# Fused attention and MLP forward and backward: the copy of turned e in block 0, q's column in parts, K's turn and k's maximum at other places, six buffers of h1

## Chip, cores and metric

One core of a Trainium2 chip runs the whole program in one launch. The metric is the device time of one execution in microseconds. Before the change the median of three runs is 2354.04 us (2353.44 to 2355.04).

## What is computed

The kernel computes an attention branch and an MLP branch on one normalized input, gates one with the other, and returns the output and the gradients of seven inputs for a given `grad_out`. Sequence 2048, width 512, 32 heads of 16, MLP width 1792, bfloat16 in and out.

```python
xn = layernorm(x)
q, k, v = split_heads(xn @ wqkv)                     # 32 heads of 16
s = (softmax(q @ k.T * 0.25) @ v) @ wo               # attention branch
g = silu(gelu(layernorm(xn) @ w1 + b1) @ w2 + b2)    # MLP branch
out = x + s * g
_, vjp = jax.vjp(f, x, wqkv, wo, w1, b1, w2, b2); grads = vjp(grad_out)
```

## The kernel before

The program has three parts: a preparation (`phase_pre`, about 0 to 175 us), the attention forward and backward together (`attention_core`, about 175 to 1970 us), and the rest of the backward pass (`phase3`).

**Preparation, first half.** Rows are normalized and projected to q, k and v in 16 tiles of 128 rows (groups `g` of four tiles). For each tile of k the squares are made on GpSimd (`norms`, L174, tile `sq`) and summed on VectorE (L175, `kn`).

**Preparation, second half**, written in the order of its engines' queues (`manual_schedule` for PE, ACT, DVE and POOL; SP's order is left to the scheduler):

- `h_tile(g, fc)`: one tile of h = y w1 in the turned layout, four matmuls (L264) for each of 4 groups and 14 chunks `fc`. The bias is added on DVE (L267) or ACT (L269) into one half of a pair tile `h1p`, of which there are four buffers. After each second chunk ACT makes the gelu of the pair (L271), and SP stores h1 and gelu(h1) (L272 `H1T_s`, L273 `HGT_s`). A buffer of `h1p` comes free when its store has landed.
- `q_norm(t)`: the squared norm of a row of q per head, squares on POOL (L174, `sq` from `NQ`), sum on DVE (L175, `qn`). Sixteen of them are strewn between the h tiles of groups 1, 2 and 3.
- k's maximum: `reduce_max` over k's norms on DVE (L457) and a `partition_all_reduce` on POOL (L458), in group 1 behind `h_tile(1, 0)`. The reduction needs another code library on POOL than the squares do: one `MODIFY_POOL_CONFIG` stands ahead of it and one ahead of the next `sq`.
- `m_group(g)`: the second MLP matmul for four row tiles (L282, 14 matmuls each), its addition of the bias on DVE (L286), sigmoid on ACT (L289, L290), and five DVE operations (L294 to L309) that give the gate's products, stored from POOL's queue (L310).
- `do_proj`, `do_done`: the gradient of the attention output (L345, L346), copied into the padded operand `QPad` (L353) and stored (L356).
- `row_shift()`: from q's norms and k's maximum a bound of each row of scores, the square root on ACT (L437), the first column of `NQ` on DVE (L438), the copy into `QPad` on POOL (L440), two DMA transposes of `QPad` into `QDT` (L426, `turn_q`, for blocks 0 and 1), the store of `NQ` (L443, 2176 KB), and the copy `NATQq` (L444). A one-element Exp (L471) behind the square root brings the exponential's table in.

Two DMAs of SP's queue matter besides: K's turn (L450, `KPad` into `KVT`, written behind `h_tile(0, 8)`), and the load of `b2` (L247), for whose conversion on POOL (L248) the queue of POOL waits.

**Attention.** 16 pairs of heads times 4 blocks of queries make 64 blocks of 16 steps. A step `g` has `s` (scores, L887), ACT's Exp to `et` (L915, called S), `d` (L909, two matmuls, one for each head, each with one PSUM buffer), the products `m1` and `m0` of `d` and `et` on DVE (L926, tile `gts`), and the sums `a1` (L946, L949) and `a2` (L959). A quarter of the exponentials for the other layout is had by turning `et` on TensorE (`E`, L871, tile `ET` in the one PSUM buffer `z`) and copying it on DVE (`eE`, L876) instead of a second Exp.

The order on PE, ACT and DVE is a written list (`PE_ORDER`, `DVE_ORDER`), but block 0 has its own from `first_block`: there is no block before it, so the last quarter of `m_group` work is done in its gaps (`left_over`: tiles 12 to 15 of the MLP product, then the rest of the `do` projections, L411, and one turn, L402). On PE step `g` of block 0 is s(g+2), [E(g-1) at g = 4, 8 and 12], d(g+1), a1(g), V, a2(g-1), W(g). V and W are the places of the left-over work: W(0) to W(7) are the halves of the products of tiles 12 to 15 (seven matmuls each, in the buffer `z`), W(8), W(9), W(11), W(12) are `do` projections. On DVE a left-over tile has its bias addition (L286), `rest1` (L294, L295, L304) and `rest2` (L308, L309). The lists are merged by a loop that gives out an instruction as soon as what it needs has been given out:

```python
            if g % 4 == 0 and g and g // 4 - 1 in turned:
                p.append(("E", g - 1))
                v.append(("eE", g - 1))
            p += [("d1", g + 1), ("d0", g + 1), ("a1", g), ("V", g)]
```

From block 1 on the written lists hold, and nothing of the change reaches them.

Of the kernel before, what the change touches and what calls it, by code (L numbers as in the profile page):

```python
# [41 lines left out]
def phase_pre(ctx, tc, k, A_x, A_wqkv, A_wo, B_w1, B_b1, B_w2, B_b2, grad_out, opnds, psz, tailp):  # L42
# [210 lines left out]
    def h_tile(g, fc):  # L253
        if fc == 0 and g < 3:
            hgT[g] = p2.tile([128, FC, 512], bf16, name="hgT")[:]
        elif fc == 0:
            hgT[g] = k.dQall[:].rearrange("p t d -> p (t d)")[:, 0:FC * 512].rearrange("p (c s) -> p c s", c=FC)
        if fc % 2 == 0:
            if g or fc:
                h1ps.append(p2.tile([128, 2, 512], bf16, name="h1p", bufs=4))  # L260
        h1p = h1ps[-1]
        ps = psA.tile([128, 512], f32, name="ps_h1", tag="mm")
        for ic in range(IC):
            nc.tensor.matmul(ps[:], lhsT=w1_sb[:, ic, fc * 128:(fc + 1) * 128], rhs=yT[g][:, :, ic, :],  # L264
                             start=(ic == 0), stop=(ic == IC - 1))
        if fc % 2 == 0 or fc in (5, 11):
            nc.vector.tensor_scalar(out=h1p[:, fc % 2], in0=ps[:], scalar1=b1c[:, fc:fc + 1], scalar2=None, op0=ALU.add)  # L267
# [161 lines left out]
    def q_norm(t):  # L429
        norms(p2, qn2[:, t, :], NQ[:, :, t, :, 1:17])  # L430

    def row_shift():

        nc.vector.tensor_scalar(out=kmax2[:], in0=kmax2[:], scalar1=UINFL, scalar2=None, op0=ALU.mult)
        nc.vector.tensor_tensor(out=qn2[:], in0=qn2[:], in1=kmax2[:].rearrange("p (o h) -> p o h", o=1).to_broadcast([128, NT, H]),
                                op=ALU.mult)
        nc.scalar.activation(out=qn2[:], in_=qn2[:], func=ACT.Sqrt)  # L437
        nc.vector.tensor_scalar(out=NQ[:, :, :, :, 0], in0=qn2[:].rearrange("p t (a j) -> p a t j", j=2), scalar1=-1.0, scalar2=None,  # L438
                                op0=ALU.mult)
        nc.gpsimd.tensor_copy(out=QPad[:, :, 0:2, 0:17], in_=NQ[:, 0])  # L440
        turn_q(0)
        turn_q(1)
        nc.sync.dma_start(out=k.NATQq_s, in_=NQ[:].rearrange("p a t j c -> p a (t j c)"))  # L443
        nc.gpsimd.tensor_copy(out=OP0["NATQq"][:], in_=NQ[:, 0])  # L444

    with tc.manual_schedule(engines={ET_.PE, ET_.Activation, ET_.DVE, ET_.Pool}):
        for fc in range(FC):
            h_tile(0, fc)
            if fc == 8:
                nc.sync.dma_start_transpose(out=OP0["KVT"][:].rearrange("r (m k) -> r m k", m=16), in_=KPad[:].rearrange("q k s c -> q (k s c)"))  # L450
        qn = list(range(NT))
        for fc in range(FC):
            h_tile(1, fc)
            if fc in (2, 4, 7, 9, 12):
                q_norm(qn.pop(0))
            if fc == 0:
                nc.vector.reduce_max(out=kmaxrun[:], in_=kn2[:].rearrange("p t h -> p h t"), axis=AX.X)  # L457
                nc.gpsimd.partition_all_reduce(kmax2[:], kmaxrun[:], channels=128, reduce_op=bass_isa.ReduceOp.max)  # L458
# [339 lines left out]
def attention_core(ctx, tc, opnds, ps_z, tail, NAT_s, NATQ_s, Oall, dQall, dKVT_out, ident_f32, ident_bf, npairs=16, nqc=4, turned=(0, 1, 2)):  # L798
# [265 lines left out]
    def first_block():  # L1064
# [16 lines left out]
    def joined(first, rest):  # L1081
# [197 lines left out]
```

## Time and profile before

| | |
|---|---|
| median of three runs | 2354.04 us (2353.44 to 2355.04) |
| profiled execution | 2355.04 us, its span 2353.3 us |
| busy: PE, DVE, ACT, POOL | 95%, 86%, 87%, 13% of the span |
| mean granted clock of TensorE | 0.985 |
| preparation, up to the first score | 0 to 175 us |
| block 0, up to the first steps of block 1 | 175 to 232 us |

Times are microseconds from the span's start. A line of the timeline gives start, busy time, engine, line, operation, output and inputs, shape and count; in brackets stands the idle time of the engine ahead of it and what ended that. Lines of the same kind close together are merged into one. PEld is the weight load of TensorE; SPq is the issue of a DMA on SP's queue. A line of the windows view gives for one stretch the busy time of PE, PEld, DVE, ACT and POOL with counts, the granted clock of TensorE as a share of full speed, the share of busy DMA, and GB/s.

### The profile page before, as it was taken

What the parts mean: (1) busy time and instruction counts of PE and PEld (TensorE: products, weight loads), DVE (VectorE), ACT (ScalarE), POOL (GpSimd) and SP (SyncE); (2) the same over time, 40 slices, a digit from 0 to 9 for tenths busy, and PEclk for the clock granted to TensorE, in tenths of its full rate; (3) what the DMA queues carried; (4) which work ended last, traced back from release to release, by engine and by line L of the source; (5) the groups of instructions that cost most, each with busy time, mean ns of one, the idle gap of its engine ahead of it and who ended that gap; (6) DMA issues with size and microseconds to landing.
All of it is one profiled execution on the core that took longest, in us unless ns stands there. A gap on an engine that the chain in (4) does not pass through costs nothing.

```text
span 2353.3 us, 50893 instructions
## 1 busy us (share of the span) xinstructions
PE 2235.4 (95%) x20082; PEld 796.2 (34%) x20128; DVE 2024.0 (86%) x3600; ACT 2043.5 (87%) x2329; POOL 314.8 (13%) x757
## 2 busy tenths in 40 slices
PE   7898999999999999999999999999999998889698
PEld 3342333333333333333333333333333333334343
DVE  6576999999999999999999999999999996775164
ACT  6564999999999999999999999999999998883143
POOL 4230111111111111111111111111111112100000
PEclk9998999999999999999999999999999999999799
DMA  9686999999999989999999999999999998796961
GB/s 288 221 276 149 176 170 173 177 165 185 158 189 163 180 163 180 163 180 175 169 177 167 184 163 183 164 179 166 177 167 173 160 155 229 192 205 129 172 161 63
DMA packets 1315362, 415.56 MB, mean 177 GB/s; under 512 B 1272241, under 2 KB 1291698, under 8 KB 1313970
## 3 DMA queue, kind: packets, MB, share of 16 engines
q1 hardware_dynamic: 1311362, 401.56, 90.0%
q0 software_dynamic: 2176, 7.34, 0.9%
q8 instruction: 157, 2.57, 0.4%
q10 hardware_dynamic: 1584, 3.41, 0.4%
q14 instruction: 83, 0.68, 0.1%
HBM read 46.52 MB, written 49.03 MB: 41 GB/s over the span
## 4 chain that ended last, share of the span: by engine, by line
PE 76%; DVE 12%; issue 3%; DMA 3%; ACT 3%; SPq 2%; POOL 0%; ACTq 0%; DVEq 0%; POOLq 0%
PE d L909 12%; PE X L946 11%; PE s L887 11%; PE Z L1027 9%; PE X L959 7%; DVE gts L926 5%; PE Z L1019 5%; PE ET L871 5%; PE t L899 4%; PE XT L971 2%; PE X L949 1%; PE ps_dy L709 1%; PE ps_dwkv L759 1%; PE ps_dw L654 1%; PE ps_m L282 1%
## 5 line engine op out<-in xcount | busy, mean ns | idle before, releaser
L926 DVE TENSOR_TENSOR gts<-d,et 128x512 bf16<-128x512 f32 x2048 | 1322.0, 684 | 77.1 <-issue 25.9
L915 ACT ACTIVATE et<-s 128x1024 bf16<-128x1024 f32 x1024 | 1044.8, 1046 | 11.4 <-PE d L909 11.1
L920 ACT ACTIVATE e<-t 128x1024 bf16<-128x1024 f32 x832 | 867.8, 1044 | 23.1 <-PE t L899 6.2
L909 PE MATMUL d<-QDT,KVT 32*128 32x512 bf16 x2048 | 757.9, 384 | 22.4 <-DVE gts L926 21.3
L887 PE MATMUL s<-QDT,KVT 32*128 32x512 bf16 x2048 | 398.1, 384 | 5.8 <-DMA QDT<-QPad 3.1
L1027 PE MATMUL Z<-gk,W 128*32 128x512 bf16 x2048 | 397.0, 384 | 0.0
L946 PE MATMUL X<-et,Lc 128*32 128x512 bf16 x2048 | 369.8, 388 | 0.0
L949 PE MATMUL X<-et,NAT 128*32 128x512 bf16 x2048 | 368.7, 388 | 0.0
L959 PE MATMUL X<-gts,NAT 128*17 128x512 bf16 x2048 | 330.9, 382 | 0.0
L1019 PE MATMUL Z<-e,W 128*32 128x512 bf16 x1664 | 321.6, 383 | 2.8 <-DVE ob L1046 1.2
L899 PE MATMUL t<-KVT,QDT 32*128 32x512 bf16 x1664 | 323.2, 383 | 1.0 <-ACT e L920 1.0
L909 PEld LDWEIGHTS <-KVT 32*128 32x128 bf16 x2048 | 173.4, 91 | 236.7 <-issue 236.3
L887 PEld LDWEIGHTS <-KVT 32*128 32x128 bf16 x2048 | 105.9, 91 | 251.0 <-issue 227.7
L993 POOL TENSOR_TENSOR W<-NATQd,rL 128x128 bf16<-128x128 bf16 x64 | 25.7, 401 | 1124.7 <-DVE rL L992 1124.7
L1027 PEld LDWEIGHTS <-W 128*32 128x32 bf16 x2048 | 100.2, 94 | 172.5 <-issue 142.2
L1019 PEld LDWEIGHTS <-W 128*32 128x32 bf16 x2048 | 105.4, 94 | 106.6 <-issue 97.3
L899 PEld LDWEIGHTS <-QDT 32*128 32x128 bf16 x1664 | 92.1, 91 | 145.7 <-issue 140.9
L946 PEld LDWEIGHTS <-Lc 128*32 128x32 bf16 x2048 | 83.5, 93 | 165.0 <-issue 164.9
L876 DVE COPY eE<-ET 128x1024 bf16<-128x1024 bf16 x192 | 130.2, 678 | 6.6 <-PE ET L871 6.6
L871 PE MATMUL ET<-ident_bf,et 128*128 128x128 bf16 x1536 | 119.1, 220 | 0.9 <-DVE e L286 0.9
L871 PEld LDWEIGHTS <-et 128*128 128x128 bf16 x1536 | 86.5, 98 | 44.4 <-issue 44.4
L959 PEld LDWEIGHTS <-NAT 128*17 128x17 bf16 x2048 | 79.6, 89 | 59.1 <-issue 42.8
(197 smaller groups left out, 2334.6 us busy)
## 6 DMA issues: line engine op xcount, KB each, us to landing
gk<-gts SPq DMA_TRANSPOSE x512, 4.5
H1T_s<-h1p SPq DMA_DIRECT2D x28, 256.0 KB, 3.7
h<-H1T_s SPq DMA_DIRECT2D x28, 256.0 KB, 3.5
HGT_s<-hgT SPq DMA_DIRECT2D x21, 256.0 KB, 4.3
NAT_s<-NS SPq DMA_DIRECT2D x4, 1056.0 KB, 5.5
dKVT_s<-ob SPq DMA_DIRECT2D x16, 256.0 KB, 3.6
gb<-GB_s SPq DMA_DIRECT2D x4, 1024.0 KB, 6.2
Rkv<-dKVT_s SPq DMA_DIRECT2D x2, 2048.0 KB, 14.7
```

What stands on the lines that cost most here:

```text
L871: nc.tensor.transpose(ET[:, hj, m * 128:(m + 1) * 128], st_et[g - 3 + m][:, hj, 384:512], ident_bf[:])
L887: nc.tensor.matmul(s[:, hj, :], lhsT=op["KVT"][r, kb * 128:(kb + 1) * 128], rhs=op["QDT"][r, qc * 512:(qc + 1) * 512], start=True, stop=Tr ...
L899: nc.tensor.matmul(t[:, hj, :], lhsT=op["QDT"][r, q0:q0 + 128], rhs=op["KVT"][r, kc * 512:(kc + 1) * 512], start=True, stop=True, tile_pos ...
L909: nc.tensor.matmul(d[:], lhsT=op["KVT"][r, kb * 128:(kb + 1) * 128], rhs=op["QDT"][r, qc * 512:(qc + 1) * 512], start=True, stop=True, til ...
L915: nc.scalar.activation(out=et[:], in_=st_s.pop(g)[:], func=ACT.Exp)
L920: nc.scalar.activation(out=e[:], in_=st_t.pop(g)[:], func=ACT.Exp)
L926: nc.vector.tensor_tensor(out=gts[:, g % 2, hj], in0=st_d.pop((g, hj))[:], in1=st_et[g][:, hj], op=ALU.mult)
L946: nc.tensor.matmul(X[64 + 32 * hj:96 + 32 * hj, :], lhsT=Lc[:, :], rhs=et[:, hj, :], start=(kb == 0), stop=False, skip_group_check=True, t ...
L949: nc.tensor.matmul(X[32 * hj:32 * hj + 32, :], lhsT=NATt[:, kb, hj, 1:33], rhs=et[:, hj, :], start=(kb == 0), stop=(kb == 15), tile_positi ...
L959: nc.tensor.matmul(X[64 + 32 * hj:64 + 32 * hj + 17, :], lhsT=NATt[:, kb, hj, 0:17], rhs=gts[:, kb % 2, hj, :], start=False, stop=(kb == 1 ...
L1019: nc.tensor.matmul(Z[32 * hj:32 * hj + 32, :], lhsT=blk[j]["W1"][:, qb, hj, :], rhs=e[:, hj, :], start=(qb == 0), stop=False, tile_positio ...
L1027: nc.tensor.matmul(cur["Z"][32 * hj:32 * hj + 32, :], lhsT=blk[j]["W2"][:, qb, hj, :], rhs=grhs, start=False, stop=(qb == 3), tile_positio ...
```

## The change

- `h1p` has six buffers instead of four.
- k's maximum (`reduce_max` and `partition_all_reduce`) stands behind `h_tile(0, 5)` instead of `h_tile(1, 0)`.
- K's turn is written behind `h_tile(1, 13)` instead of `h_tile(0, 8)`.
- The `q_norm`s are spread 6, 6 and 4 over groups 1, 2 and 3 instead of 5, 5 and 6.
- `row_shift` is split: the two multiplications on DVE behind `h_tile(3, 9)`, the square root behind `h_tile(3, 13)` and so ahead of the last `do_proj` copy, the column of `NQ` and the copy into `QPad` in two parts (tiles 0 to 3, tiles 4 to 15) behind the small Exp, each with its turn. The store of `NQ` is written behind `m_group(2)`.
- In block 0 `eE(g-1)` stands in DVE's list behind the products `m(g)`, not ahead of them.

The order of PE's instructions is the same in both. SP's scheduler puts K's turn at the same place as before, right ahead of the load of `b2`. The store of `NQ` and the reload behind it (L830 before, L837 after) now stand behind the two turns of `QPad`, and ahead of the turn of `dso` (L299). On POOL the reduction's first library now comes right behind the conversion of `b2`, and the two copies into `KPad` for the second pair (L834 and L835 before) come between the squares. In block 0 the loop now gives out m(4), m(8) and m(12) one step earlier: m(4) stands ahead of `rest2` of tile 12 and of the bias addition of tile 13, m(8) ahead of `rest2` of tile 14 and of the bias addition of tile 15.

```diff
-    h1ps = [p2.tile([128, 2, 512], bf16, name="h1p", bufs=4)]
+    h1ps = [p2.tile([128, 2, 512], bf16, name="h1p", bufs=6)]
...
-    def row_shift():
+    def row_shift1():
...
+    def row_shift2():
         nc.scalar.activation(out=qn2[:], in_=qn2[:], func=ACT.Sqrt)
...
-        nc.gpsimd.tensor_copy(out=QPad[:, :, 0:2, 0:17], in_=NQ[:, 0])
-        turn_q(0)
-        turn_q(1)
-        nc.sync.dma_start(out=k.NATQq_s, in_=NQ[:].rearrange("p a t j c -> p a (t j c)"))
+    def row_shift3():
+        for ts in (slice(0, 4), slice(4, 16)):
+            nc.vector.tensor_scalar(out=NQ[:, :, ts, :, 0], in0=qn2[:, ts].rearrange("p t (a j) -> p a t j", j=2), scalar1=-1.0, scalar2=None,
+                                    op0=ALU.mult)
+            nc.gpsimd.tensor_copy(out=QPad[:, ts, 0:2, 0:17], in_=NQ[:, 0, ts])
+            turn_q(ts.start // 4)
...
             h_tile(0, fc)
-            if fc == 8:
-                nc.sync.dma_start_transpose(out=OP0["KVT"][:]...)
+            if fc == 5:
+                nc.vector.reduce_max(out=kmaxrun[:], in_=kn2[:].rearrange("p t h -> p h t"), axis=AX.X)
+                nc.gpsimd.partition_all_reduce(kmax2[:], kmaxrun[:], channels=128, reduce_op=bass_isa.ReduceOp.max)
...
             h_tile(1, fc)
-            if fc in (2, 4, 7, 9, 12):
+            if fc in (2, 4, 6, 8, 10, 12):
                 q_norm(qn.pop(0))
-            if fc == 0:
-                nc.vector.reduce_max(...)
-                nc.gpsimd.partition_all_reduce(...)
+        nc.sync.dma_start_transpose(out=OP0["KVT"][:]...)
...
+                if g == 3 and fc == 9:
+                    row_shift1()
+                if g == 3 and fc == FC - 1:
+                    row_shift2()
                 if fc >= 10:
                     do_proj(4 * (g - 2) + fc - 10)
-                elif fc in (1, 3, 5, 6, 8) or fc == 9 and g == 3:
+                elif fc in (1, 3, 5, 6) or fc in (8, 9) and g == 2:
                     q_norm(qn.pop(0))
...
-        row_shift()
         e_one = ...
+        row_shift3()
         m_group(2)
+        nc.sync.dma_start(out=k.NATQq_s, in_=NQ[:].rearrange("p a t j c -> p a (t j c)"))
...
                 p.append(("E", g - 1))
-                v.append(("eE", g - 1))
...
             v += [("m1", g), ("m0", g)]
+            if ("E", g - 1) in p:
+                v.append(("eE", g - 1))
```

More of the change, by code (lines that the diff above doesn't have):

```diff
@@ L259, in h_tile @@
             if g or fc:
-                h1ps.append(p2.tile([128, 2, 512], bf16, name="h1p", bufs=4))
+                h1ps.append(p2.tile([128, 2, 512], bf16, name="h1p", bufs=6))
         h1p = h1ps[-1]
@@ L436, in row_shift @@
                                 op=ALU.mult)
+    def row_shift2():
         nc.scalar.activation(out=qn2[:], in_=qn2[:], func=ACT.Sqrt)
-        nc.vector.tensor_scalar(out=NQ[:, :, :, :, 0], in0=qn2[:].rearrange("p t (a j) -> p a t j", j=2), scalar1=-1.0, scalar2=None,
-                                op0=ALU.mult)
-        nc.gpsimd.tensor_copy(out=QPad[:, :, 0:2, 0:17], in_=NQ[:, 0])
-        turn_q(0)
-        turn_q(1)
-        nc.sync.dma_start(out=k.NATQq_s, in_=NQ[:].rearrange("p a t j c -> p a (t j c)"))
+    def row_shift3():
[4 more added lines that the diff above has]
+            turn_q(ts.start // 4)
         nc.gpsimd.tensor_copy(out=OP0["NATQq"][:], in_=NQ[:, 0])
@@ L448, in phase_pre @@
             h_tile(0, fc)
-            if fc == 8:
-                nc.sync.dma_start_transpose(out=OP0["KVT"][:].rearrange("r (m k) -> r m k", m=16), in_=KPad[:].rearrange("q k s c -> q (k s c)"))
+            if fc == 5:
+                nc.vector.reduce_max(out=kmaxrun[:], in_=kn2[:].rearrange("p t h -> p h t"), axis=AX.X)
+                nc.gpsimd.partition_all_reduce(kmax2[:], kmaxrun[:], channels=128, reduce_op=bass_isa.ReduceOp.max)
         qn = list(range(NT))
@@ L453, in phase_pre @@
             h_tile(1, fc)
-            if fc in (2, 4, 7, 9, 12):
+            if fc in (2, 4, 6, 8, 10, 12):
                 q_norm(qn.pop(0))
-            if fc == 0:
-                nc.vector.reduce_max(out=kmaxrun[:], in_=kn2[:].rearrange("p t h -> p h t"), axis=AX.X)
-                nc.gpsimd.partition_all_reduce(kmax2[:], kmaxrun[:], channels=128, reduce_op=bass_isa.ReduceOp.max)
+        nc.sync.dma_start_transpose(out=OP0["KVT"][:].rearrange("r (m k) -> r m k", m=16), in_=KPad[:].rearrange("q k s c -> q (k s c)"))
         m_group(0)
```

## Prediction

> **What bounds the kernel now.** I read the page first, then the windows by stage, then the chain of waits from 60 to 240 us, then the timeline of each engine there.
>
> ```profile
> span 2353.3 us, 50893 instructions
> ...
> 400.00:1800.00 1400.00, 1386.21 (x14293) 457.68 (x14291) 1343.58 (x2264) 1383.81 (x1492) 187.77 (x520) 1.00 1.00 173
> ```
>
> From 400 to 1800 us TensorE is busy 1386 of 1400 us at full clock, and the order there is not touched. So the change is worth what it brings block 1 forward, no more. The profiled execution took 2355.04 us against its span of 2353.3, and the median of the runs, 2354.04, is 1.0 below it. I take the differences off the median; 0.2% of it, 4.7 us, is about what a measurement tells from no change.
>
> Three places ahead of block 1 carry the argument. The first is a stop of all engines around 90 us (timeline rows, the two library changes from the view of their lines).
>
> ```profile
> 78.30 0.61 POOL L248 CAST b2f<-b_bf 128x512 f32<-128x512 bf16 x1 [10.59 <-DMA b_bf<-in_B_b_dram]
> L458 POOLq MODIFY_POOL_CONFIG  x2: 15/15/15, 82.3 to 82.3; - x2
> 85.66 1.03 DVE L457 TENSOR_REDUCE kmaxrun<-kn 128x32 f32<-128x512 f32 x1
> 88.19 0.45 POOL L458 PARTITION_ALL_REDUCE kmax<-kmaxrun  x1 [5.86 <-DVE h1p L267]
> L174 POOLq MODIFY_POOL_CONFIG  x2: 99/99/99, 88.6 to 88.6; - x2
> 96.42 4.12 POOL L174 TENSOR_TENSOR sq<-NQ 128x512 f32<-128x512 bf16 x4 [7.78 <-issue]
> 97.48 0.69 DVE L175 TENSOR_REDUCE qn<-sq 128x32 f32<-128x512 f32 x1 [10.13 <-POOL sq L174]
> 81.15 11.34 PE L264 MATMUL ps_h<-yT,w_sb 128*128 128x512 bf16 x44 [3.84 <-DVE h1p L267]
> 98.88 4.19 PE L264 MATMUL ps_h<-yT,w_sb 128*128 128x512 bf16 x12 [6.39 <-DVE h1p L267]
> ```
>
> POOL changes its library at 82.3, reduces at 88.19, changes back at 88.6 and makes the first square at 96.42. DVE stands 10.13 us behind that square with the additions of h1 queued behind it, and so PE stands 6.39 us. The reduction's input was ready at 85.66 + 1.03 = 86.69, 1.5 us ahead of its start, and the second change, which waits for nobody's data, also takes 7.8 us; so I read the 5.86 as the library, though the profile names DVE.
>
> **k's maximum and the six buffers.** The new order puts the first library change right behind the conversion of b2, done at 78.30 + 0.61 = 78.91. K's turn keeps its place ahead of that load on SP's queue, so I give it no effect. Input is then ready early (its DVE time of 1.03 us lies in waits). The same lengths give: reduction at 78.91 + 5.86 = 84.8, first square 96.42 - 88.19 = 8.23 later, at 93.0 instead of 96.42: **3.4 us**. What follows is as before: the sum on DVE, the addition behind it, the last three tiles on PE (12 matmuls in 4.19 us, cold). The two copies into KPad now lie between the squares; PE then needs the gelus of group 0 only, so they hide behind m_group(0). A sixth sum each in groups 1 and 2 (0.69, group 3 has two fewer) I put at 0, at worst 0.7 twice. The second pair's turn of K slips behind two turns of q; block 4 is the first to use it.
>
> The six buffers take away the 3.84 us wait of PE for stores of h1 at 81.15, but the tile that stops at the square is the same (the seven PSUM buffers end there), so PE only arrives earlier at that stop: 0. If the stop were gone they would be worth up to 3.84. The cover is the stop itself. For the libraries no row shows a load at 79 us; the nearest bounds are 1.5 us (if 88.19 was the reduction's answer to its input) and 5.86 for the first, and for the end no later than 96.42, since DMA was as busy at 82 us. So 0 to 7.8 us; I take 3.4 by the row of the same instruction.
>
> A rule of the Trainium skill (GPSIMD Engine Reference, Instruction dispatch) puts the first call into a freshly loaded library at about 6 us, 5.95 measured; taken for both loads it would give a gain nearer 5 than 3.4. The trace has 5.86 for the first and more for the second.
>
> **q's column in parts, its store later.**
>
> ```profile
> 162.76 0.57 ACT L346 CAST ND<-pd 128x512 bf16<-128x512 f32 x1
> 165.30 1.30 DVE L438 TENSOR_SCALAR NQ<-qn 128x512 bf16<-128x512 f32 x1 [4.70 <-ACT qn L437]
> 166.64 0.32 SPq L443 DMA_DIRECT2D NATQq_s<-NQ  x1
> 166.67 0.67 POOL L440 COPY QPad<-NQ 128x544 bf16<-128x544 bf16 x1 [2.75 <-DVE NQ L438]
> 174.11 0.32 SPq L830 DMA_DIRECT2D NATQq<-NATQq_s  x1
> 175.07 0.39 PE L887 MATMUL s<-QDT,KVT 32*128 32x512 bf16 x2 [3.08 <-DMA QDT<-QPad]
> 175.82 2.83 ACT L915 ACTIVATE et<-s 128x1024 bf16<-128x1024 f32 x3
> 178.10 2.02 SPq L299 DMA_TRANSPOSE QDT<-dso  x1
> 181.29 0.39 SPq L317 DMA_DIRECT2D gk<-in_grad_out_dram  x1
> 188.78 0.42 DVE L295 TENSOR_TENSOR gk<-gk 128x512 bf16<-128x512 bf16 x1
> NATQq_s<-NQ SPq DMA_DIRECT2D x1, 2176.0 KB, 7.5
> gk<-in_grad_out_dram SPq DMA_DIRECT2D x1, 512.0 KB, 5.9
> ```
>
> PE waits 3.08 us for QDT, whose turns were queued behind the 2176 KB store of NQ. That wait goes, but the first Exp at 175.82 comes directly, without idle, behind the last sigmoid of m_group(2) on ACT, and that sigmoid hangs on DVE, whose chain starts with the column at 165.30. The square root moves ahead of one copy (0.57), so the chain starts some 0.5 us earlier; against this the new DVE order puts two gate operations of the last tile ahead of the first product of block 0. I take 0 for this part. Its bounds are +3.1 (the wait, if the Exp could follow) and -1.
>
> The store now goes out behind both turns, about 5 us later than 166.64, and lands 7.5 later, near 179.2. SP's head, the reload at 174.11, then waits there until then; queued behind it are the turn and store of dso and the load of grad_out for tiles 12 to 15. The turn had waited for DVE until 178.10 anyway, so the load slips from 181.29 to about 182.6 and lands 5.9 later, at 188.5. DVE first uses it at 188.78. I take -0.2.
>
> **Block 0.**
>
> ```profile
> 186.94 1.68 PE L282 MATMUL ps_m<-Oall,dQall 128*128 128x512 bf16 x7
> 189.43 1.69 PE L282 MATMUL ps_m<-Oall,dQall 128*128 128x512 bf16 x6
> 191.15 0.69 DVE L286 TENSOR_TENSOR e<-ps_m,b2f 128x512 bf16<-128x512 f32 x1 [0.42 <-PE ps_m L282]
> 191.89 0.61 PE L871 MATMUL ET<-ident_bf,et 128*128 128x128 bf16 x8 [0.46 <-DVE e L286]
> 192.54 0.69 DVE L876 COPY eE<-ET 128x1024 bf16<-128x1024 bf16 x1 [0.70 <-PE ET L871]
> 193.88 1.18 PE L909 MATMUL d<-QDT,KVT 32*128 32x512 bf16 x2 [1.38 <-DVE gts L926]
> 195.96 3.17 PE L282 MATMUL ps_m<-Oall,dQall 128*128 128x512 bf16 x7
> 200.57 1.78 PE L282 MATMUL ps_m<-Oall,dQall 128*128 128x512 bf16 x7
> 210.09 0.37 PE L909 MATMUL d<-QDT,KVT 32*128 32x512 bf16 x1 [1.38 <-DVE gts L926]
> 211.95 3.12 PE L411 MATMUL pd<-KVT,QDT 128*128 128x512 bf16 x8
> 216.17 1.89 PE L411 MATMUL pd<-KVT,QDT 128*128 128x512 bf16 x7 [0.24 <-ACT gk L412]
> 226.32 0.37 PE L909 MATMUL d<-QDT,KVT 32*128 32x512 bf16 x1 [1.38 <-DVE gts L926]
> 227.76 3.29 PE L411 MATMUL pd<-KVT,gk 128*128 128x512 bf16 x8
> ...
> 190.00:193.50 3.50, 1.99 (x15) 1.00 (x14) 2.35 (x5) 1.70 (x4) 0.54 (x1) 1.00 0.80 188
> 207.40:210.80 3.40, 1.33 (x12) 0.71 (x10) 2.70 (x5) 2.26 (x3) 0.37 (x1) 1.00 0.40 113
> 221.00:224.40 3.40, 2.16 (x13) 0.88 (x13) 0.00 (x0) 2.33 (x3) 0.00 (x0) 1.00 0.93 141
> 224.40:227.80 3.40, 1.79 (x17) 0.70 (x18) 2.82 (x5) 1.64 (x2) 0.00 (x0) 1.00 0.48 90
> ```
>
> A plain step takes 189.43 - 186.94 = 2.49 us. Each of the three turns of e costs PE a wait of 1.38 us: d cannot start until the products of the step are made, and these are queued behind the copy eE, which waits for the turn. Behind each wait seven or eight matmuls take 3.12 to 3.29 us instead of 1.69: the clock has fallen to half. The windows view shows what precedes it: stretches with 1.99, 1.33 and 1.79 us of PE work in 3.4 to 3.5 us lose the clock; the one with 2.16 keeps it.
>
> In the new order the products are made a step earlier, so d follows the turn at once. At the first two turns the products and two operations of rest2 now lie ahead of the bias addition that frees the buffer for the turn, two products of 0.62 and so 1.25 us more on DVE, of which the 0.42 us idle ahead of 191.15 takes part: the turn starts 0.8 later. Waits won: 0.6, 0.6, and 1.38 at the third, which has no addition ahead of it: **2.5 us**.
>
> Then the clock. From d to the next left-over burst the first turn took 200.57 - 193.88 = 6.7 us; at full clock two short groups (2 x 0.8) and one burst (1.7) are 3.3: 3.4 won. The second took 216.17 - 210.09 = 6.1; short groups 0.8, burst 1.7, and the 1.1 us that ACT's copy takes until the next burst are 3.65: 2.4. The third, 227.76 + 3.29 - 226.32 = 4.7, against 0.9 + 1.7: 2.1. Together **7.9 us, if the clock holds in all three**. With the new order PE's idle time within 3.4 us of a turn is about 1.2, that is 2.2 us of work, just above the stretch that kept its clock. A margin that thin holds not always: I count two of three, 5.3.
>
> The Trainium skill (TensorE: Matmul & The Clock Gate, Why this matters for your kernels) speaks against this term: only gaps of more than about 3 us should lower the clock. Here it fell behind single gaps of at most 1.38 us, with 39 to 57% of the stretch busy, so the trace goes by the share, not by the gap.
>
> **The sum.** 3.4 + 0 - 0.2 + 2.5 + 5.3 = 11.0 us: 2354.04 - 11.0 = **2343.0 us**.
>
> **Rivals.**
> 1. The clock falls at the turns all the same, because the stretches around them stay thin whatever the order. Then 3.4 + 2.5 - 0.2 = 5.7: 2348.3 us. For it: 2.2 against 2.16 is no margin. Against: the fullest stretch that lost its clock had 1.99. By the clock rule of the Trainium skill above the time would be this one too.
> 2. DVE becomes the bound of block 0. Steps 4 to 7 give DVE about 11.5 us of work, PE 10.6. If every product is late by what eE gave, only the library's 3.4 is left: 2350.6, no change that can be told. Against it: DVE has idle time in each stretch above.
> 3. The reduction had answered its input and not the library: then the first square comes at 78.91 + 1.5 + 8.23 = 88.6, 7.8 us earlier, and the total is 15.4: 2338.6. For it: the profile names DVE as releaser. Against: 1.5 us is far longer than other waits between DVE and POOL here.
> 4. Slower: the store of NQ stops SP. The reload at SP's head holds the load of grad_out; from a landing at 179.4 on, each us later is one us that DVE stands at its first use at 188.78, with the products of step 4 and the bias addition behind it, and PE loses its clock too. At a landing near 190 the gain is eaten; at 195 the kernel is slower by 4.7 us, 2358.7. For it: DMA is loaded there. Against: the same store took 7.5 us, not 23.
>
> **How the numbers follow.** My forecast (two or three turns keep the clock) has 0.52, rival 1 0.24, rival 2 0.08, rival 3 0.08, rival 4 with what no row shows 0.08. Rival 1 lies close to the line of 4.7 us; a third of it and nearly all of rival 2 count as the same: faster 0.77, same 0.15, slower 0.08. The range reaches from rival 3 with all three clocks held (7.8 + 2.5 + 7.9 - 0.2 = 18.0 us, and 1 of the column's 3.1) to rival 2 with the column's -1: 2335 to 2351.5; rival 4 is left out, and the far ends of 3.
>
> **What would show it.** The profile after should have: the library change at about 79 and the first square at 93, with PE's stop at the tile products still there; the first score near 172 minus 3.4 but the first Exp only some 3.4 us earlier than 175.82; no wait of d for gts behind the turns; bursts of 1.7 us behind at least two turns; block 1 some 11 us earlier. I am wrong if the first square stays at 96, if the first scores are much earlier than that with Exp following, if the bursts stay at 3.2 us, or if DVE waits for grad_out.

## The result, and the profile after

The changed kernel takes 2340.27 us in the median of four runs (2337.01 to 2342.74), the kernel before beside it 2353.74 (2351.28 to 2355.04): a ratio of 0.9943, with an interval of 0.9926 to 0.9960. Run once more later it took 2340.76 us against 2352.30, a ratio of 0.9948 (0.9934 to 0.9961). So it is faster by 11.5 to 13.5 us; the forecast was 11.0, 2343.0 us.

The profiled execution was the fastest of the four, 2337.01 us with a span of 2335.1, and that of the kernel before the slowest of its four, so the two traces differ by 18.2 us, more than the change is worth. This table cuts both spans, and that of the second trace of the changed kernel, at the same instructions (us):

| stretch | before | changed | changed, second trace |
|---|---|---|---|
| start to the conversion of b2 | 78.30 | 76.75 | 78.37 |
| to the first product of group 0 | 24.60 | 20.96 | 21.75 |
| to the first product of group 2 | 56.84 | 56.82 | 56.84 |
| to the left-over burst ahead of the first turn, W(3) | 29.69 | 30.19 | 30.24 |
| to the last score of block 0 | 41.56 | 30.98 | 30.99 |
| to XT of block 2 | 34.74 | 36.66 | 36.65 |
| to the first turn of o behind attention | 1686.7 | 1686.0 | 1685.9 |
| to the end of the span | 400.9 | 396.7 | 398.0 |

Rows two to six are where the change works: 11.8 us are gained there in the first trace, 11.0 in the second. The first row is when b2 happens to land, and the last part is not touched by any edit: over all fourteen traces of this study it took 396.2 to 402.7 us in no order that goes with the edits.

The stop behind the libraries in the changed kernel: the first library change from the view of its line (first and last start stand behind the durations), then the timeline of POOL, DVE and PE.

```profile
L454 POOLq MODIFY_POOL_CONFIG  x2: 11/11/11, 77.3 to 77.3; - x2
```

```profile
76.75 0.61 POOL L248 CAST b2f<-b_bf 128x512 f32<-128x512 bf16 x1 [10.42 <-DMA b_bf<-in_B_b_dram]
69.60 1.01 DVE L453 TENSOR_REDUCE kmaxrun<-kn 128x32 f32<-128x512 f32 x1
83.10 0.45 POOL L454 PARTITION_ALL_REDUCE kmax<-kmaxrun  x1 [5.73 <-DVE h1p L267]
90.85 2.03 POOL L174 TENSOR_TENSOR sq<-NQ 128x512 f32<-128x512 bf16 x2 [7.30 <-DMA HGT_s<-hgT]
81.68 4.48 PE L264 MATMUL ps_h<-yT,w_sb 128*128 128x512 bf16 x20 [0.18 <-DVE h1p L267]
93.31 4.56 PE L264 MATMUL ps_h<-yT,w_sb 128*128 128x512 bf16 x12 [7.15 <-DVE h1p L267]
97.71 12.25 PE L282 MATMUL ps_m<-Oall,hgT 128*128 128x512 bf16 x54
```

The library change now begins at 77.3, as the conversion ends. The reduction's input has been ready since 70.6, and still it starts 5.8 us behind that change: the wait is the library, whatever releaser the row names. The 3.84 us wait for stores of h1 is gone, and the stop at the square grew from 6.39 to 7.15.

The three turns of e in block 0, in PE's timeline:

```profile
184.72 1.69 PE L282 MATMUL ps_m<-Oall,dQall 128*128 128x512 bf16 x6
187.81 0.61 PE L878 MATMUL ET<-ident_bf,et 128*128 128x128 bf16 x8 [1.08 <-DVE e L286]
188.34 0.39 PE L916 MATMUL d<-QDT,KVT 32*128 32x512 bf16 x2
189.21 1.69 PE L282 MATMUL ps_m<-Oall,dQall 128*128 128x512 bf16 x7
199.90 0.61 PE L878 MATMUL ET<-ident_bf,et 128*128 128x128 bf16 x8 [1.05 <-DVE e L286]
201.30 1.90 PE L411 MATMUL pd<-KVT,QDT 128*128 128x512 bf16 x8
213.86 1.90 PE L411 MATMUL pd<-KVT,gk 128*128 128x512 bf16 x8
215.70 0.39 PE L894 MATMUL s<-QDT,KVT 32*128 32x512 bf16 x2
```

d follows the turn at once, with no idle time in brackets. The bursts take 1.69 and 1.90 us where they took 3.12 to 3.29. What is left is the wait ahead of the first two turns, 1.08 and 1.05 us.

Ahead of block 0 and at the start of block 1 two rows, the DVE one and XT, show costs that the kernel before did not have. SP's and POOL's rows show an order that changed there, first in the changed kernel, then in the kernel before:

```profile
171.65 0.42 DVE L294 TENSOR_TENSOR gB<-m,sg 128x512 bf16<-128x512 bf16 x1 [0.79 <-DMA GB_s<-gB]
219.62 3.63 SPq L849 DMA_TRANSPOSE KVT<-KPad  x1
225.75 0.63 SPq L838 DMA_DIRECT2D NATQd<-NATQd_s  x1
230.02 0.61 POOL L846 COPY QPad<-NATQd 128x512 bf16<-128x512 bf16 x1 [9.17 <-DMA NATQd<-NATQd_s]
224.28 1.11 PE L978 MATMUL XT<-ident_f,xs 128*128 128x128 f32 x4
```

```profile
231.09 1.93 SPq L842 DMA_TRANSPOSE KVT<-KPad  x1
238.99 0.57 SPq L831 DMA_DIRECT2D NATQd<-NATQd_s  x1
241.98 0.61 POOL L839 COPY QPad<-NATQd 128x512 bf16<-128x512 bf16 x1 [4.62 <-DMA NATQd<-NATQd_s]
```

DVE waits 0.79 us for a buffer of gB, that is for the landing of an earlier GB_s store. K's turn for the second pair now stands closer ahead of the reload of dO on SP's queue: a turn of q and the store of dO that stood between them now go out first, and one turn of `gts` is left between. POOL's copy of dO waits 9.17 us for the reload instead of 4.62. XT of block 1 takes 1.11 us where it took 0.66: the clock is down there, from 219.9 to 226.7, which it was not at this place before.

### The profile page after: what moved, and what is told of

Read it like the earlier page. It is cut to its first block, busy times and chain, and to the rows that moved or that the text cites. A ratio compares the mean times of both kernels' runs of the same rounds, so it can differ in the third digit from the quotient of the medians.

```text
span 2335.1 us, 50892 instructions
## 1 busy us (share of the span) xinstructions
PE 2228.5 (95%) x20082; PEld 795.2 (34%) x20128; DVE 2024.3 (87%) x3601; ACT 2043.9 (88%) x2329; POOL 315.3 (14%) x758
## 3 DMA queue, kind: packets, MB, share of 16 engines
q10 hardware_dynamic: 1584, 3.41, 0.4%
## 4 chain that ended last, share of the span: by engine, by line
PE 77%; DVE 10%; ACT 3%; issue 3%; DMA 3%; SPq 2%; POOL 0%; DVEq 0%; ACTq 0%; POOLq 0%
PE d L916 12%; PE X L953 11%; PE s L894 11%; PE Z L1034 9%; PE X L966 7%; DVE gts L933 5%; PE Z L1026 5%; PE t L906 5%; PE ET L878 5%; PE XT L978 2%; PE ps_dw L661 1%; PE X L956 1%; PE ps_dhg L676 1%; PE ps_dy L716 1%; PE ps_dwkv L766 1%
```

## The experiments

**Block 0 alone.** The kernel before with the new place of eE:

```diff
-                v.append(("eE", g - 1))
             ...
             v += [("m1", g), ("m0", g)]
+            if ("E", g - 1) in p:
+                v.append(("eE", g - 1))
```

> The kernel before with the new place of eE in block 0 and nothing else. My theory: the products ahead of the copy take PE's wait for d away at all three turns and the clock then holds. From the first matmul of the left-over burst ahead of the first turn to the last score of block 0 the kernel before takes 230.99 - 189.43 = 41.6 us, the changed one 215.70 - 184.72 = 31.0; so this one takes about 31, all bursts behind the turns take 1.7 to 1.9 us, and the time is about 9 us under the kernel before (10.6, less up to 2 that the start of block 1 may give back). Rival A: the turns kept their clock in the changed kernel because the earlier edits had moved them in time; then at least one burst stays at 3.1 to 3.3 us, and the gain is 7 us or less. Rival B: most of the changed kernel's gain came from ahead of block 0; then the gain here is under 4 us.

It took 2346.43 us against 2353.83, a ratio of 0.9968 (0.9956 to 0.9980): 7.4 us. PE's and POOL's timeline:

```profile
189.81 1.69 PE L282 MATMUL ps_m<-Oall,dQall 128*128 128x512 bf16 x6
194.23 1.69 PE L282 MATMUL ps_m<-Oall,dQall 128*128 128x512 bf16 x7
206.32 1.90 PE L411 MATMUL pd<-KVT,QDT 128*128 128x512 bf16 x8
218.88 1.90 PE L411 MATMUL pd<-KVT,gk 128*128 128x512 bf16 x8
220.72 0.39 PE L887 MATMUL s<-QDT,KVT 32*128 32x512 bf16 x2
234.89 0.61 POOL L839 COPY QPad<-NATQd 128x512 bf16<-128x512 bf16 x1 [9.10 <-DMA NATQd<-NATQd_s]
237.35 0.39 PE L1019 MATMUL Z<-e,W 128*32 128x512 bf16 x2 [1.68 <-POOL W L998]
```

From W(3) to the last score it takes 30.9 us, and all three bursts are at full clock, at other places of the span than in the changed kernel: both rivals fall. But 4.2 of the 10.7 us won, and not up to 2 as expected, are lost again in block 1. PE's first Z there waits 1.68 us for the weights W, which are queued on POOL behind the copy of dO that waits 9.10 us for its reload, and the clock is at half for 6.8 us behind that. K's turn has its new place on SP's queue here too, so the edit of block 0 is enough to bring it.

**k's maximum alone.** The kernel before with `reduce_max` and `partition_all_reduce` behind `h_tile(0, 5)`:

```diff
+            if fc == 5:
+                nc.vector.reduce_max(out=kmaxrun[:], ...)
+                nc.gpsimd.partition_all_reduce(kmax2[:], kmaxrun[:], ...)
...
-            if fc == 0:        # the same two lines behind h_tile(1, 0)
```

> The kernel before with k's maximum behind the sixth tile of h instead of the fifteenth, four buffers of h1 and all else as before. My theory: POOL starts the first library change right behind the conversion of b2 and everything from the reduction on comes 3.4 to 4 us earlier: first square at about 92.5 to 93 where the kernel before has 96.42, PE's wait of 3.84 us for the stores of h1 still there, the time 3.4 us (2.5 to 4.5) under the kernel before. Rival A: the reduction had answered its input and not the library; then the first square comes 7 to 8 us earlier and the time falls by 7. Rival B: the six buffers were needed for it, PE comes too late to use the earlier square; then the time falls by under 1 us.

It took 2348.70 us, a ratio of 0.9979 (0.9969 to 0.9988): 5.1 us less, more than the 2.5 to 4.5 expected, though the interval of 2.8 to 7.3 takes in most of them. POOL's and PE's timeline:

```profile
78.11 0.61 POOL L248 CAST b2f<-b_bf 128x512 f32<-128x512 bf16 x1 [10.86 <-DMA b_bf<-in_B_b_dram]
92.80 2.03 POOL L174 TENSOR_TENSOR sq<-NQ 128x512 f32<-128x512 bf16 x2 [7.94 <-issue]
80.96 11.33 PE L264 MATMUL ps_h<-yT,w_sb 128*128 128x512 bf16 x44 [6.07 <-DVE h1p L267]
95.26 4.10 PE L264 MATMUL ps_h<-yT,w_sb 128*128 128x512 bf16 x12 [2.97 <-DVE h1p L267]
```

From b2's conversion to the first square it is 14.7 us instead of 18.1: 3.4 us, the value of the forecast. One trace of each does not hold it so closely: with block 0's edit alone, which leaves this place as it was, it is 17.3. The wait for stores of h1 was longer than expected, 6.07 us, and the stop behind it shorter: together they went from 10.2 to 9.0 us.

**Four buffers, and the old column.** The changed kernel with `bufs=4` for `h1p`; and with `row_shift` and the store of NQ as before:

```diff
-    h1ps = [p2.tile([128, 2, 512], bf16, name="h1p", bufs=6)]
+    h1ps = [p2.tile([128, 2, 512], bf16, name="h1p", bufs=4)]
```

```diff
-    def row_shift1(): ...        # and row_shift2, row_shift3, at their three places
+    def row_shift(): ...         # column whole, then NQ's copy, turn_q(0), turn_q(1)
+        nc.sync.dma_start(out=k.NATQq_s, in_=NQ[:]...)     # on SP's queue ahead of the two turns
...
         m_group(2)
-        nc.sync.dma_start(out=k.NATQq_s, in_=NQ[:]...)
```

> The changed kernel with four buffers of h1 instead of six. My theory: PE's wait for the stores of h1 comes back (3 to 4 us near 80), and its stop behind the first square, 7.15 us in the changed kernel, gets as much shorter: the first product of group 0 stays at 97.7 and the time within 1 us of the changed kernel. Rival: the buffers were worth their wait; then the first product comes 3 to 4 us later, and so does the end.

> The changed kernel with q's column whole, its square root and the store of NQ at the places of the kernel before (store ahead of the turns of QPad). My theory: this part moves almost nothing. The first Exp of block 0 comes about 0.7 us later than in the changed kernel, counted from the first product of group 2, because the chain on DVE starts later; but DVE no longer waits 0.79 us for a buffer of gB and the first product of block 0 again comes ahead of the last gate operations, so that the first left-over burst is within 1 us of the changed kernel, and the time within 1.5 us. Rival A: PE's wait of 3 us for the turns decides; then the time is 3 us longer. Rival B: the store behind the turns cost more than it gave (the wait for gB, the two gate operations); then the time is 1 to 2 us shorter.

They took 2344.14 and 2342.89 us against 2353.83 before, ratios of 0.9951 (0.9939 to 0.9963) and 0.9950 (0.9937 to 0.9963), which does not part them from the changed kernel's 0.9943 and 0.9948. PE's timeline with four buffers, then PE's and ACT's with the old column:

```profile
80.21 11.29 PE L264 MATMUL ps_h<-yT,w_sb 128*128 128x512 bf16 x44 [4.20 <-DVE h1p L267]
94.06 4.29 PE L264 MATMUL ps_h<-yT,w_sb 128*128 128x512 bf16 x12 [2.56 <-DVE h1p L267]
```

```profile
171.78 0.39 PE L886 MATMUL s<-QDT,KVT 32*128 32x512 bf16 x2 [3.75 <-DMA QDT<-QPad]
172.21 2.86 ACT L914 ACTIVATE et<-s 128x1024 bf16<-128x1024 f32 x3 [0.53 <-PE d L908]
176.88 1.46 PE L282 MATMUL ps_m<-Oall,dQall 128*128 128x512 bf16 x3
```

With four buffers the wait is 4.20 us and the stop 2.56 instead of 7.15, in sum the same: the six are worth nothing as long as the stop stands. With the old column PE waits 3.75 us for QDT, the first Exp comes 16.4 us behind the first product of group 2 instead of 15.3, and yet the first left-over burst comes after 21.1 us (176.88 - 155.78) against 21.3 (175.79 - 154.53). What the column's parts win at the Exp is gone at the burst. One point of the expectation missed: DVE still waits for gB, 0.63 us instead of 0.79. So the place of NQ's store is not what makes that wait, which the kernel before and those with block 0's edit or k's maximum alone do not have (20.64 or 20.65 us to the burst). The traces show what differs: the store whose landing frees the buffer takes 6.06 to 6.25 us in the kernels that wait and 4.85 to 5.11 in those three, and DVE comes to the buffer 0.2 to 0.7 us earlier. Why the store takes longer stays open; of the edits, the new spread of the `q_norm`s had no run of its own.

**The stop itself.** k's maximum behind the second tile of h, the conversion of b2 behind the first square of q, with six and with four buffers:

```diff
-    nc.gpsimd.tensor_copy(out=b2f[:], in_=b2_bf[:])      # ahead of the tiles of h
...
-            if fc == 5:                                   # k's maximum, group 0
+            if fc == 1:
...
+            if fc == 3:                                   # group 1, behind the first q_norm
+                nc.gpsimd.tensor_copy(out=b2f[:], in_=b2_bf[:])
```

> The changed kernel (2340.3) with k's maximum behind the second tile of h and ahead of the conversion of b2, which goes behind the first square; both library changes then lie before the first square is needed. My theory: the stop of all engines is the two library changes alone. The first square then comes near 80 instead of 90.85, PE's wait of 7.15 us for it goes and the last three tiles run at full clock; the 28 tiles of groups 0 and 1 run at the 0.91 us per tile that the changed kernel has up to the stop, and the first product of group 0 comes 8 to 9 us earlier than at 97.71: time near 2332. Rival A: something else lies right behind the stop (the stores of h1, the gelus on ACT, the load of w2); then PE waits elsewhere and under 4 us are won. Rival B: the stop is no matter of libraries; then the first square stays near 91 and nothing is won.

> The same kernel as e5_early but with four buffers of h1. My theory: with the stop gone nothing hides the wait for the stores of h1 any more, and six buffers are worth that wait: PE stands 3 to 4 us or more near 80, the first product of group 0 comes 3 to 5 us later than in e5_early, and so does the end. Rival: the buffers are worth nothing in this order either; then the two agree within 1 us.

With six buffers 2330.85 us against 2351.08, 0.9915 (0.9902 to 0.9928); with four 2335.93, 0.9940 (0.9928 to 0.9952). POOL's and PE's timeline with six, then PE's with four:

```profile
82.93 1.03 POOL L174 TENSOR_TENSOR sq<-NQ 128x512 f32<-128x512 bf16 x1 [9.60 <-DMA H1T_s<-h1p]
82.80 7.07 PE L263 MATMUL ps_h<-yT,w_sb 128*128 128x512 bf16 x32 [0.19 <-DVE h1p L266]
89.70 12.25 PE L281 MATMUL ps_m<-Oall,hgT 128*128 128x512 bf16 x56
```

```profile
81.33 14.12 PE L263 MATMUL ps_h<-yT,w_sb 128*128 128x512 bf16 x56 [6.76 <-DVE h1p L266]
95.29 12.25 PE L281 MATMUL ps_m<-Oall,hgT 128*128 128x512 bf16 x56
```

The wait behind the second library change was longer, 9.6 us, so the first square came at 82.93 and not near 80; but PE runs all 28 tiles of h without a stop, and the first product comes 8.0 us earlier than in the changed kernel. Rivals A and B fall. By XT of block 2, 1.7 of the 8.0 us are lost again; PE's first Z of block 1 waits 1.60 us for W here. With four buffers PE stands 6.76 us behind DVE, which waits for the stores: without the stop to hide behind, two buffers are worth 5.1 us.

**The gate operations and gB.** `rest2` of a left-over tile behind `second` of the next, and `gB` with four buffers:

```diff
-            steps[2 * n + 3][0].append((rest2, t))
+        for n, t in enumerate(range(12, 16)):
+            steps[2 * n + 3][1].append((rest2, t))
...
-            gB = p2.tile([128, 2, D], bf16, name="gB", bufs=3)[:]
+            gB = p2.tile([128, 2, D], bf16, name="gB", bufs=4)[:]
```

> The changed kernel with the two last gate operations of each left-over tile written behind the bias addition of the next one, and four buffers of gB instead of three. My theory: PE's waits of 1.08 and 1.05 us ahead of the first two turns of block 0 are these two operations (0.41 + 0.42 us) on DVE, and DVE's wait of 0.79 us is the third buffer of gB: both turns come 0.4 to 0.6 us earlier after the first left-over burst, this burst 0.8 us earlier after the first product of group 2, and the time falls by 1 to 2 us under the changed kernel. Rival: the operations only come due later, and the next step waits for them instead; then the distance from the first burst to block 1 stays at 39.5 us and nothing is won there.

2336.05 us against 2351.08, 0.9941 (0.9926 to 0.9955), no difference from the changed kernel that can be told. PE's timeline:

```profile
189.17 0.61 PE L879 MATMUL ET<-ident_bf,et 128*128 128x128 bf16 x8 [0.46 <-DVE e L286]
232.81 0.48 PE L1027 MATMUL Z<-e,W 128*32 128x512 bf16 x2 [1.23 <-POOL W L1006]
```

Both mechanisms are there: the waits at the first two turns fall to 0.46 us (the first is shown), and the first burst comes 20.4 us (177.10 - 156.71) behind the first product of group 2 instead of 21.3. In this trace it is given back at once: at the start of block 1 Z waits 1.23 us for W, and the clock falls behind that. The six runs lie far apart, three at 2333.4 to 2333.8 us and three at 2338.3 to 2342.6, and the traced one took 2342.64; whether the others lost as much there is not shown.

**The reload of dO on POOL**, for the second pair alone:

```diff
-            nc.sync.dma_start(out=t["NATQd"][:]...)
+            (nc.gpsimd if p == 1 else nc.sync).dma_start(out=t["NATQd"][:]...)
```

> The changed kernel with the reload of dO for the second pair issued by POOL instead of SP, for that pair alone. In the changed kernel K's turn of the second pair stands right ahead of this reload on SP's queue, where it stood two places earlier before; POOL's copy of it into QPad then waits 9.17 us, with the weights W of block 0 queued behind it, for which PE's first Z waits (1.68 us in the run with block 0's edit alone, and the clock falls behind it). My theory: the copy comes about 2 us earlier, no wait of Z for POOL is left in block 1, and the two blocks from the first left-over burst to the last turn of block 1 take 0 to 3 us less than in the changed kernel, more where the clock had fallen behind that wait. Rival: the clock falls at the start of block 1 for the short waits of d for DVE (0.33, 0.20 and 0.59 us) alone; then nothing changes there, and the time stays within 1 us.

2340.97 us against 2351.08, 0.9956 (0.9944 to 0.9967): nothing won. POOL's copy comes at 227.57 with a wait of 2.38 us instead of 230.02 with 9.17, so the queue works as thought; but in this trace too the clock had fallen before XT of block 1 (XT took 1.11 us), and a slow PE reaches Z after W in any case. The rival holds for the changed kernel.

**The changed kernel again, all three together, and a dose of waiting.** The first is without an edit, the second has the three diffs above together (k's maximum and b2 with six buffers, `rest2` and gB, the reload); the dose is the changed kernel with

```diff
         def rest2(t):
+            if t in (12, 14):
+                q, sg, gB, m = v[t]
+                for _ in range(2):
+                    nc.vector.tensor_tensor(out=gB[:, 1, :], in0=sg, in1=do4[3][:, t % 4, :], op=ALU.mult)
             m_grad2(t, *v[t][0:3])
```

> The changed kernel once more, as a second trace and a measure beside the next one. My theory: what the first trace gained ahead of the changed part (its tiles of h began 1.56 us earlier) and behind attention (4.2 us) is chance, what it gained between is not. So from the first tile of h to the first turn of o behind attention it takes the same as in the first trace within 2 us (1874.9, against 1887.3 before), and the time is 11 to 14 us under the kernel before. Rival: the gain outside the changed part is caused by the change; then it is there again, 5 to 6 us.

> The edits of e5_early, e7_rest2 and e8_padq together on the changed kernel. My theory: the stop behind the libraries goes (8 us, of which 1.5 to 2 are given back by lower clock at the start of blocks 0 and 1, as in e5_early), the first two turns come 0.6 us earlier each and the first burst of block 0 0.8 us, and with the reload of dO on POOL the first Z of block 1 waits for no weights: 8 to 9 us under the changed kernel, 20 to 23 under the kernel before. Rival: what the turns win is given back at the start of block 1, by ACT's pace or by the clock, as in e7_rest2; then it is no faster than e5_early, 6 to 7 us under the changed kernel.

> The changed kernel with two more operations on DVE (0.42 us each, the last gate operation done twice more with the result thrown away) ahead of the bias additions that the first two turns of block 0 wait for. PE's waits there grow from 1.08 and 1.05 to about 1.9 us. If the clock goes by the share of work in a stretch of 3.4 us, some 1.5 to 1.9 us of work are left in it, under the 1.99 with which the kernel before lost its clock: the bursts behind both turns take 3.1 to 3.2 us instead of 1.7 and 1.9, and from the first burst of tile 13 to the last score of block 0 it takes 6 to 8 us longer than the 31.0 of the changed kernel. If only gaps of over 3 us lower the clock, the bursts stay at 1.7 to 1.9 us and it takes 1.7 us longer.

The second trace of the changed kernel is the last column of the table. The time fits; the length that I had named missed by 0.9 us (1877.8, not 1874.9 within 2), as b2 landed later behind the first tile of h. Of the 5.8 us gained outside the changed part 2.8 came again, all of it behind attention, which is within what this part does by itself.

The three edits together took 2326.54 us against 2352.30, 0.9886 (0.9872 to 0.9899): 25.8 us under the kernel before and 14.2 under the changed kernel beside it, more than either theory gave and more than the three gave alone. Against the kernel with the stop removed, its trace is 1.9 us ahead at W(3) and 3.5 more at XT of block 2: the turns wait 0.46 us, Z of block 1 waits for nothing, and from the start of block 0 to 270 us the clock is at half once only, up to 169.5 us. So what the turns won, which the trace of `rest2` alone lost to the clock at the start of block 1, is kept here. From the last score of block 0 to XT of block 2 it takes 35.1 us, against 36.7 in the changed kernel and 34.7 in the kernel before. This is the fastest version of the study.

The dose: PE's timeline, and two stretches of the windows view, cut where the clock can change, which in each trace is only at steps of 3.41 us (the last section):

```profile
188.46 0.77 PE L882 MATMUL ET<-ident_bf,et 128*128 128x128 bf16 x8 [1.89 <-DVE e L286]
190.67 2.41 PE L282 MATMUL ps_m<-Oall,dQall 128*128 128x512 bf16 x7
202.67 0.61 PE L882 MATMUL ET<-ident_bf,et 128*128 128x128 bf16 x8 [1.82 <-DVE e L286]
204.07 1.90 PE L415 MATMUL pd<-KVT,QDT 128*128 128x512 bf16 x8
```

```profile
185.34:188.76 3.42, 1.53 (x13) 0.68 (x11) 3.00 (x7) 0.32 (x1) 0.54 (x1) 1.00 0.52 100
198.99:202.41 3.42, 1.86 (x9) 0.68 (x8) 3.35 (x8) 0.54 (x1) 0.10 (x1) 1.00 0.72 138
```

One run took 2345.13 us. The waits are as meant, 1.89 and 1.82 us. The clock fell behind the first turn and held behind the second; to the last score it takes 33.9 us, 2.9 more than the changed kernel, between the two expectations. Nearly equal gaps ended differently: the first lay in a stretch with 1.53 us of work, the second in one with 1.86.

**Without the reload on POOL**, all else as in the three together:

> The kernel e9_joined with the reload of dO for the second pair back on SP's queue behind K's turn, and nothing else changed. My theory: wherever the clock has not fallen at the start of block 1 already, PE's first Z there waits for the weights W that stand on POOL behind this reload (1.23 to 1.68 us in four earlier traces), and the clock falls behind that wait; in e9_joined, where the reload is on POOL, neither was there. So here the wait of 1.2 to 1.7 us is back, with 3.4 to 6.8 us at half clock behind it, and the time is 2 to 4.5 us above e9_joined's 0.9886 of the kernel before. Rival: that e9_joined kept its clock there was a matter of where its work fell in time; then the wait is back without a fall, and the time within 1.5 us of it.

2332.42 us against 2352.49, 0.9913 (0.9899 to 0.9926). PE's timeline:

```profile
223.17 0.39 PE L1028 MATMUL Z<-e,W 128*32 128x512 bf16 x2 [1.27 <-POOL W L1007]
225.51 0.60 PE L1028 MATMUL Z<-e,W 128*32 128x512 bf16 x2
```

Wait and slow clock are back (the second Z takes 0.60 us), so the rival falls. From XT of block 1 to XT of block 2 it takes 29.75 us against 27.56 in the kernel with the reload on POOL (27.18 in the kernel before). That is 2.2 us; the ratios differ by 6.3 us. The traces have the rest ahead of XT of block 1 (1.4, of which 1.3 are there before group 0's products) and behind attention (2.8), where no order differs, so how much of it is the edit's stays open.

## Why the prediction was right, point by point

**The libraries, 3.4 us: right.** The first change moved ahead of the two copies into KPad and the wait before them, and the reduction followed 5.8 us later with its input ready for 12.5 us. The stretch from b2's conversion to the first product gained 3.6 and 2.9 us, k's maximum alone 3.4 to the square. The sixth `q_norm` in group 2 cost nothing: from group 0 to group 2 it takes 56.8 us in both kernels. Rival 3, the reduction answering its input, is refuted by the same rows. The Trainium skill (GPSIMD Engine Reference, Instruction dispatch) gives about 6 us for the first call behind such a change, and the runs agree, with 5.55 to 6.09 us. For the way back they show more, 6.9 to 9.8 us of waiting ahead of the first square.

**Six buffers, 0, the cover being the stop: right**, from both sides: 4.20 + 2.56 us instead of 0.18 + 7.15 with the stop, and 5.1 us of time without it.

**q's column, 0 within -1 and +3.1: right.** From group 2 to W(3) the changed kernel takes 0.5 us more. The two gate operations ahead of the first product had been named; the wait of 0.79 us for gB had not, and in the run with four buffers of gB the burst came 0.9 us earlier.

**The store of NQ, -0.2: nothing was lost, but not by the way that was worked out.** The store landed by 170.93, 7.0 us behind its issue. It had gone out 2.5 us later than before, counted from the first product of group 2, and not 5, so SP was free again before the turn of `dso`, and the load of grad_out went out 21.3 us behind that product against 21.6 before. The slip of 1.3 us did not come, and rival 4 did not come about.

**Block 0's waits, 2.5 us: right, and the clock, 5.3: too small.** All three turns held the clock, in every trace with the new order but the dose. From W(3) to the last score 10.6 us went. The waits won are 0.76, 0.79 and 1.38 us, 2.9 in all, which leaves 7.7 for the clock: close to the 7.9 worked out before one turn in three was struck off for a thin margin. Rivals 1 and 2 are refuted. The 2.2 against 2.16 had been read from stretches that did not begin and end where the clock can change. Cut there, the stretch that holds the first turn has 2.34 us of work where before it had 1.58, and those of the other two have 2.9 and 2.6 where before they had 1.3 and 1.8. At the first turn the margin was thin all the same: another stretch of this trace, shown below, lost the clock with 2.29.

**What was not in the sum: 1.9 us lost at the start of block 1.** The loss hid the undersized clock term, so that the total fits (3.6 or 2.9 - 0.5 + 10.6 - 1.9, that is 11.8 or 11.0, for 11.0) better than its parts: that closeness is luck. Two steps lack in the working. The first goes with the 1.9 us: thin stretches were looked for at the turns only, and not in the block that comes forward. With all three edits, where the clock held there and Z did not wait, only 0.4 us are lost at this place. Stretches of the windows view, cut where the clock can change, before and then after:

```profile
190.56:193.98 3.42, 1.58 (x14) 0.85 (x13) 2.30 (x5) 2.08 (x3) 0.54 (x1) 1.00 0.63 157
221.28:224.70 3.42, 2.38 (x16) 1.18 (x18) 0.00 (x0) 2.35 (x3) 0.00 (x0) 1.00 0.93 131
```

```profile
185.75:189.17 3.42, 2.34 (x22) 0.92 (x19) 2.69 (x7) 1.35 (x3) 0.54 (x1) 1.00 0.64 156
216.47:219.88 3.41, 2.29 (x20) 0.67 (x18) 2.94 (x5) 3.10 (x4) 0.53 (x2) 1.00 0.96 185
219.88:223.30 3.42, 2.70 (x22) 0.72 (x19) 2.58 (x4) 2.86 (x4) 0.67 (x1) 0.50 1.03 235
```

In the stretch from 216.47 d waits three times for DVE, 2.29 us of work are left, and the next one runs at 0.50; one with 2.38 before, and one with 2.34 at the first turn, kept their clock. The second is "the second pair's turn of K slips behind two turns of q; block 4 is the first to use it". I asked who uses the turn, and not what is queued behind it on SP, whose order no written list gives: the reload of dO, behind that a copy on POOL, behind that the weights of block 0, and behind those Z on PE. In the changed kernel the clock falls ahead of that wait, Z comes later and does not wait, and the reload on POOL won nothing; where it does not fall there, as with block 0's edit alone and in the version without the reload, the wait of 1.3 to 1.7 us comes, and the clock falls behind it. That the thin stretch makes the clock fall there is read from these rows; no run changed it alone.

## What to carry to other kernels

When an edit lets a DMA slip in its queue, follow not only the one who reads it but the whole queue behind it, through each engine that waits, to the engine that sets the end. A wait that another wait hides is worth nothing until the other goes, and then all at once: look for the last stop in the stage first, and make the others' edits after it. And compare traces stretch by stretch between the same instructions: two traces of one kernel differed by 3.6 us here, and the first trace of the changed kernel gained 6.4 us in parts where the change does not work.

## What the runs showed of the hardware

The slow stretches of TensorE's clock lie on a fixed grid: in each trace they begin and end whole multiples of 3.41 us apart (before they begin at 176.9, 194.0, 211.0 and 228.1, each five steps from the last) and last one to three steps. The Trainium skill (TensorE: Matmul & The Clock Gate, Part 1) has a free-running window of that length, and the traces agree. The Trainium skill (TensorE: Matmul & The Clock Gate, Why this matters for your kernels) wants gaps of over about 3 us for a fall, and there they differ: of the grid's stretches at full clock between 60 and 270 us in the fourteen traces, each with up to 1.35 us of work was followed by half clock, and none with over 2.29. Between the two both occur. Nearly the same gap can hold the clock or lose it by where the grid cuts it, as in the dose (1.86 and 1.53 us of work). At the end of the products of group 2, large matmuls of 128 rows, nine traces kept the clock with 1.43 to 2.32 us, of which 1.43 to 1.98 were of the large ones; two lost it with 1.54 and 1.62, of which 0.8 and 0.7 were. At the start of block 1, mostly small matmuls of 32 rows, eight lost it with 2.00 to 2.29. That looks as if the small ones counted for less, but it was not tested by itself.
